# Soft-MoE routing behind beacon attention: logits in four column groups, dispatch turned on VectorE, combine rows replicated at the output

## Chip, cores and metric

The kernel runs on one core of a Trainium2 chip. The metric is the device time of one execution in microseconds; the number shown for a kernel is the median of its runs. A profile is of one execution, and its span runs from the first to the last instruction.

## The reference, cut to what matters

```python
# attention: B, H, S, Nb, D = 8, 8, 576, 16, 64
k_all = np.concatenate([beacon_k, k], axis=2)
v_all = np.concatenate([beacon_v, v], axis=2)
scores = 1/np.sqrt(D) * np.matmul(q, k_all.transpose(0, 1, 3, 2))
scores = np.where(causal, -1e9, scores)        # beacons are always seen
a = softmax(scores)                            # over the keys
x = np.matmul(a, v_all)                        # -> (B*S, H*D) = (4608, 512)
# soft MoE: 8 experts, 4 slots each (32 slots), F = 1024
logits = x @ phi                               # (4608, 32)
d = softmax(logits, over tokens)               # dispatch
slot_input = d.T @ x                           # (32, 512), 4 rows per expert
slot_out[e] = np.maximum(slot_input[e] @ w1[e], 0) @ w2[e]
c = softmax(logits, over slots)                # combine
return c @ slot_out                            # (4608, 512), fp32
```

The dispatch normalization needs the logits of all tokens of all batches, so the experts start only after the last attention output. The kernel takes the exponential of the logits once and without a maximum; dispatch and combine both use it, and divide by the sums over tokens (`dsum`, `rd`) and over slots (`csp`, `rc`).

## The kernel before

**Attention.** The 64 heads go in 32 pairs, `n` = 0 to 31; four pairs make a batch (`b, g = divmod(n, 4)`). A pair's tokens, 16 beacons ahead of 576, are five chunks of 128 (the last 80). Q and K are loaded by SP in fp32 into five rotating buffers of `arena`; `transp` turns them on PE (L265), and VectorE or ScalarE copies the result to `qT` and `kT` (L269, L271); GpSimd copies the beacons' K (L258). `score` has four stages `s0` to `s3`: matmuls into one of two double banks `scs` (L282), one exponential on ScalarE (L289), and the causal mask on GpSimd (L291). `attend_head` multiplies by V with a column of ones (L304) into `av`, and `normalize` (L314, L315) writes fp16 tokens-by-features `xb`. V is loaded by GpSimd and cast; VectorE turns it block by block (`turn_v`, L151, four calls per batch).

**Routing.** `xt_piece` turns `xb` on PE (L330) to features-by-tokens `xT` (L338). `logit_piece` multiplies by `phih`, which holds phi four times side by side, so that the 128 output partitions are the 32 slots four times (L344, 288 tokens at a time); ScalarE writes the exponential to `eLh` and the sum over tokens to `dsum9` (L348). `dt_piece` turns 32 rows of `eLh` on PE (L356), and VectorE copies them to tokens-by-slots `dT` (L361 to L363). `si_products` multiplies `dT` by `xb` in four column groups (L382), and `add_si` adds to `siacc` on VectorE (L388). `col_sums` sums over the slots with a column of ones (L416).

**Order.** The kernel is scheduled by hand: each engine runs its instructions in the order of the program text. Steps 0 to 5 are written out in `head(n)`; from step 6 on a step is the list of operations in L529, run by `step`. Logits of a batch are taken in steps 2 and 3 of the next, its dispatch in step 0 of the one after, its slot product in step 1; for the last two batches they are earlier. PSUM tiles of `ps_tr` (tag `tr`) rotate over two buffers. Expert weights are loaded by GpSimd, so many per step (`want`, L561).

**Tail.** After the last step the last pair is attended in `scs[0]` and normalized, its tokens are turned, the last logits are taken, and the dispatch and slot product of batch 7 follow (`si_half`, L370), added to the folded `siacc` (`fold_si`, L397) into `siz` (L616). `warm_tail` keeps PE busy between. Then come two layers of experts, two at a time (`first_layer` L642, `turn_hidden` L650, `second_layer` L656), and the scaled slot outputs `soh` (L675).

**Output.** For each group `cg` of 512 tokens four matmuls (L687) multiply columns of `eLh`, all 128 partitions, by `soh`, whose four partition groups hold partial sums of the slots; ScalarE (L689) and VectorE (L691) scale by `rc` in turn, and SP stores 1 MB (L695, L697).

Of the kernel before, what the change touches and what calls it, by code (L numbers as in the profile page):

```python
# [17 lines left out]
def kernel(  # L18
# [13 lines left out]
    P = 128  # L32
# [181 lines left out]
    nc.vector.memset(ones[:, :], 1.0)  # L214
# [8 lines left out]
    eLh = const.tile([P, Nb + N + P - UL], F16, name="eLh")  # L223
    nc.vector.memset(eLh[:, Nb + N:], 0.0)
    nc.vector.memset(eLh[:, 0:Nb], 0.0)
    dsum9 = const.tile([P, 2 * B - 1], FP, name="dsum9")
    siz = const.tile([P, E, NDC, NSL], F16, name="siz")
    fold = const.tile([P, NSL], FP, name="fold")
    siT = const.tile([P, NDC, NSL], FP, name="siT")
    phih = const.tile([P, NDC, 4, NSL], F16, name="phih")  # L230
# [89 lines left out]
    xT = {}  # L320
    dT = {}

    def xt_piece(n, act=False):
        b, g = divmod(n, H // 2)
        if g == 0:
            xT[b] = exq.tile([P, NDC, U], F16, name="xT", tag="xT", bufs=2)
        tp = ps_tr.tile([P, NCH, P], F16, name="tr", tag="tr")
        for i in range(NCH):
            m = P if i < 4 else UL
            nc.tensor.transpose(  # L330
                tp[:, i, 0:m],
                xb[b % 2][0:m, i, 2 * g:2 * g + 2, :].rearrange("p h d -> p (h d)"),
                idh[0:m, 0:m])
        src = tp[:, :, :].rearrange("p i u -> p (i u)")[:, 0:U]
        if act:
            nc.scalar.activation(xT[b][:, g, :], src, AF.Copy)
        else:
            nc.vector.tensor_copy(out=xT[b][:, g, :], in_=src)  # L338

    def logit_piece(b, hf):  # L340
        lp = ps_tr.tile([P, 512], FP, name="tr", tag="tr")
        w = S // 2
        for t in range(NDC):
            nc.tensor.matmul(lp[:, 0:w], phih[:, t, :, :].rearrange("p g s -> p (g s)"),  # L344
                             xT[b][:, t, Nb + hf * w:Nb + (hf + 1) * w],
                             start=(t == 0), stop=(t == NDC - 1))
        o = Nb + b * S + hf * w
        nc.scalar.activation(eLh[:, o:o + w], lp[:, 0:w], AF.Exp,  # L348
                             accum_out=dsum9[:, 2 * b + hf:2 * b + hf + 1])

    def dt_piece(b):
        dT[b] = sml.tile([P, NCH, NSL], F16, name="dT", tag="dT", bufs=2)
        tp = ps_tr.tile([P, NCH, NSL], F16, name="tr", tag="tr")
        for i in range(NCH):
            m = P if i < 4 or b == B - 1 else UL
            nc.tensor.transpose(tp[0:m, i, :], eLh[0:NSL, b * S + P * i:b * S + P * i + m],  # L356
                                idh[0:NSL, 0:NSL])
        if b == B - 1:
            nc.vector.tensor_copy(out=dT[b][:, :, :], in_=tp[:, :, :])
        else:  # L360
            nc.vector.tensor_copy(out=dT[b][:, 0:4, :], in_=tp[:, 0:4, :])  # L361
            nc.vector.tensor_copy(out=dT[b][0:UL, 4, :], in_=tp[0:UL, 4, :])
        nc.vector.memset(dT[b][0:Nb, 0, :], 0.0)  # L363
# [43 lines left out]
    csp = av[:, 0, 400:512]  # L407
    rc = const.tile([P, NG * G], FP, name="rc")

    def etok(cg, j):  # L410
        o = Nb + cg * P * G
        return eLh[:, o:o + P * G].rearrange("p (t j) -> p t j", j=G)[:, :, j]

    def col_sums(c0, c1):
        for i in range(c0 * G, c1 * G):
            nc.tensor.matmul(csp[:, i:i + 1], etok(i // G, i % G)[0:NSL], ones[0:NSL, :],  # L416
                             start=True, stop=True)

    def head(n):
# [5 lines left out]
        for x, y in {1: ((0, 0), (0, 1)), 3: ((1, 1),), 4: ((1, 0), (1, 2))}.get(n, ()):  # L425
            turn_v(x, y)
# [31 lines left out]
        if n >= 2:  # L458
# [4 lines left out]
            normalize(x)  # L463
        if n == 4:
# [10 lines left out]
    def step(op, n, b, g):  # L475
        m = n + 2
        last = b == B - 1
# [13 lines left out]
        elif op == "C" and g == 2 and b > 1:  # L491
            col_sums(b - 2, b - 1)
# [6 lines left out]
        elif op == "lg" and not last and g > 1:  # L499
            logit_piece(b - 1, g - 2)  # L500
        elif op == "lL" and last and 0 < g < 3:
            logit_piece(b - 1, g - 1)
        elif op == "dt":
            if g == 0 and b > 1:
                dt_piece(b - 2)
            if n == NP - 1:
                dt_piece(b - 1)
        elif op == "si":
            if g == 1 and b > 1:
                add_si(si_products(b - 2))  # L510
            if n == NP - 1:
                add_si(si_products(b - 1))
# [11 lines left out]
    for n in range(NP):  # L524
# [3 lines left out]
        else:  # L528
            for op in ("s0", "s1", "Tq", "Tk", "s2", "V", "C", "a0", "dt", "s3", "lg", "xt", "lL",  # L529
                       "si", "a1"):  # L530
                step(op, n, b, g)

        if n == 4:
            nc.gpsimd.tensor_copy(out=phih[:, :, :, :],
                                  in_=phif[:, :, :].unsqueeze(2).broadcast_to([P, NDC, 4, NSL]))
# [5 lines left out]
        if n == 16:  # L541
            nc.gpsimd.tensor_copy(out=fold[:, :], in_=idb[:, 0:NSL])
            for z in range(1, 4):
                nc.gpsimd.tensor_tensor(out=fold[:, :], in0=fold[:, :],
                                        in1=idb[:, NSL * z:NSL * z + NSL], op=AL.add)
            nc.gpsimd.tensor_scalar(out=fold[:, :], in0=fold[:, :], scalar1=2.0 ** -8,
# [22 lines left out]
    def col_sum_factors():  # L569
        nc.vector.tensor_scalar(out=rc[:, :], in0=csp[:, 0:NG * G], scalar1=2.0 ** 8,  # L570
                                scalar2=None, op0=AL.mult)
        nc.vector.reciprocal(out=rc[:, :], in_=rc[:, :])

# [3 lines left out]
    for rows in ((4,), (3, 2, 1), (0,)):  # L577
        for a in range(2):
# [3 lines left out]
    lps = [scs[1][:, hf, 0:S // 2] for hf in range(2)]  # L582

    def last_logits(ts):
        for hf in range(2):
            for t in ts:
                o = Nb + hf * (S // 2)
                nc.tensor.matmul(lps[hf], phih[:, t, :, :].rearrange("p g s -> p (g s)"),
                                 xT[L][:, t, o:o + S // 2],
                                 start=(t == 0), stop=(t == NDC - 1))  # L590

    last_logits([0, 1])
    fold_si(0)
    xt_piece(NP - 1)
    last_logits([2])
    fold_si(1)
    last_logits([3])
    for hf in range(2):
        o = Nb + L * S + hf * (S // 2)
        nc.scalar.activation(eLh[:, o:o + S // 2], lps[hf], AF.Exp)  # L600
    col_sums(6, 7)

    def warm_tail(k):
        for _ in range(k):
            nc.tensor.matmul(scs[0][:, 1, :], idh[:, :], xT[L][:, 0, 0:512],
                             start=True, stop=True)

    warm_tail(3)
    dt_piece(L)
    warm_tail(2)  # L610
    ds = siz[:, :, :, :]
    for hf in range(2):
        sp = si_half(L, hf)
        for r in range(2):
# [8 lines left out]
    dsum = const.tile([P, 1], FP, name="dsum")  # L623
    rd = const.tile([P, 1], FP, name="rd")
    nc.vector.reduce_sum(out=dsum9[:, 2 * L:2 * L + 1], in_=eLh[:, Nb + L * S:Nb + N],
                         axis=mybir.AxisListType.X)
    nc.vector.reduce_sum(out=dsum[:, :], in_=dsum9[:, :], axis=mybir.AxisListType.X)
    nc.vector.tensor_scalar(out=dsum[:, :], in0=dsum[:, :], scalar1=2.0 ** -16, scalar2=None,
                            op0=AL.mult)
    nc.vector.reciprocal(out=rd[:, :], in_=dsum[:, :])  # L630
# [31 lines left out]
    for p in range(EP + 2):  # L662
        if p < EP:
            first_layer(p)
        if p == 1:
            col_sums(7, NG)
            col_sum_factors()
# [12 lines left out]
    for cg in range(NG):  # L680
# [15 lines left out]
        if cg > 0:  # L696
            nc.sync.dma_start(out=dst, in_=osb[:, :, :])  # L697

# [29 lines left out]
```

## Time and profile before

| | us |
|---|---|
| median of 4 runs (194.45 to 196.72) | 195.99 |
| the profiled execution | 196.72 |
| its span | 194.7 |
| busy: PE / VectorE / ScalarE / GpSimd | 156.4 / 136.4 / 130.2 / 111.1 |
| start of score 0 of pair 31 | 146.58 |
| end of the loop's last `av` matmuls | 150.87 |
| first layer starts | 157.12 |
| `soh` starts | 166.39 |
| first output issued by SP | 168.26 |
| last VectorE copy of the output ends | 180.2 |

How to read it: PE is TensorE's matmul unit, PEld its weight load, DVE VectorE, ACT ScalarE, POOL GpSimd, SP the engine that issues loads and stores. A row of a group of instructions gives line, engine, operation, output and input with shapes, the count, busy time and mean ns of one. In the timeline a line gives start, duration, engine, line, operation and, in brackets, the idle time ahead of it and who ended it. An engine that is idle costs time only if the work that sets the end stands behind it.

### The profile page before, as it was taken

What the parts mean: (1) busy time and instruction counts of PE and PEld (TensorE: products, weight loads), DVE (VectorE), ACT (ScalarE), POOL (GpSimd) and SP (SyncE); (2) the same over time, 40 slices, a digit from 0 to 9 for tenths busy, and PEclk for the clock granted to TensorE, in tenths of its full rate; (3) what the DMA queues carried; (4) which work ended last, traced back from release to release, by engine and by line L of the source; (5) the groups of instructions that cost most, each with busy time, mean ns of one, the idle gap of its engine ahead of it and who ended that gap; (6) DMA issues with size and microseconds to landing.
All of it is one profiled execution on the core that took longest, in us unless ns stands there. A gap on an engine that the chain in (4) does not pass through costs nothing.

```text
span 194.7 us, 7205 instructions
## 1 busy us (share of the span) xinstructions
PE 156.4 (80%) x3061; PEld 107.5 (55%) x3061; DVE 136.4 (70%) x283; ACT 130.2 (67%) x190; POOL 111.1 (57%) x285
## 2 busy tenths in 40 slices
PE   6688958899899789997988899899988999787000
PEld 2345746667667557775766577577655754332000
DVE  5348378699978789997878779889845552799000
ACT  2679744689969678886878698698978222598000
POOL 8659847697887587769857766677646200000000
PEclk9955888999999999999999999999999999999655
DMA  5999999999999999999999999999999991199995
GB/s 192 247 225 333 291 242 318 259 268 266 289 262 265 263 295 274 271 255 315 258 259 264 284 290 268 274 205 169 215 214 214 214 211 32 56 404 416 417 426 226
DMA packets 20464, 50.84 MB, mean 261 GB/s; under 512 B 5456, under 2 KB 5456, under 8 KB 19408
## 3 DMA queue, kind: packets, MB, share of 16 engines
q0 software_dynamic: 8048, 21.74, 56.8%
q1 hardware_dynamic: 12240, 28.35, 40.1%
q8 instruction: 24, 0.39, 0.8%
q10 hardware_dynamic: 144, 0.29, 0.5%
q14 instruction: 8, 0.07, 0.1%
HBM read 62.65 MB, written 9.44 MB: 370 GB/s over the span
## 4 chain that ended last, share of the span: by engine, by line
PE 48%; DMA 18%; DVE 8%; ACT 8%; issue 5%; POOL 3%; SPq 1%; DVEq 0%; ACTq 0%
DMA arena<-in_k_dram 14%; PE av L304 14%; PE sc L282 12%; ACT ex L289 7%; PE tr L330 4%; PE tr L265 4%; DMA vbuf<-in_v_dram 4%; PE tr L344 3%; DVE arena L691 3%; PE av L656 2%; PE sc L642 2%; DVE xb L315 2%; PE tr L382 2%; POOL ex L291 1%; PE fp L687 1%
## 5 line engine op out<-in xcount | busy, mean ns | idle before, releaser
L289 ACT ACTIVATE ex<-sc 128x736 f16<-128x736 f32 (+1 forms) x124 | 101.9, 870 | 30.2 <-PE sc L282 26.2
L291 POOL TENSOR_SCALAR_AFFINE_SELECT ex<-ex 128x256 f16<-128x256 f16 (+1 forms) x155 | 57.9, 400 | 34.9 <-ACT ex L289 34.4
L282 PE MATMUL sc<-qT,kT 64*128 64x336 bf16 (+5 forms) x384 | 43.4, 296 | 9.7 <-ACT ex L289 4.1
L304 PEld LDWEIGHTS <-ex 128*128 128x128 f16 (+1 forms) x930 | 36.0, 107 | 12.3 <-issue 11.6
L304 PE MATMUL av<-vh,ex 128*128 128x65 f16 x840 | 38.3, 198 | 3.6 <-DVE xb L315 1.8
L265 PE MATMUL tr<-idb,arena 64*64 64x64 bf16 x1152 | 28.3, 200 | 5.3 <-DMA arena<-in_k_dram 2.7
L265 PEld LDWEIGHTS <-arena 64*64 64x64 bf16 x1152 | 23.4, 113 | 13.5 <-issue 9.0
L271 DVE COPY qT<-tr 128x576 bf16<-128x576 bf16 x32 | 24.0, 749 | 5.9 <-PE tr L265 5.8
L315 DVE TENSOR_TENSOR xb<-av,r 128x640 f16<-128x640 f32 x31 | 25.6, 824 | 1.1
L282 PEld LDWEIGHTS <-kT 64*128 64x128 bf16 (+1 forms) x384 | 16.5, 101 | 16.8 <-issue 6.5
L338 DVE COPY xT<-tr 128x592 f16<-128x592 f16 x31 | 14.1, 460 | 13.0 <-PE tr L330 12.8
L151 DVE STREAM_TRANSPOSE vh<-vbuf 128x256 f32<-128x256 f32 x32 | 20.4, 659 | 3.2 <-DMA vbuf<-in_v_dram 3.1
L271 DVE COPY kT<-tr 128x576 bf16<-128x576 bf16 x27 | 20.2, 750 | 3.3 <-PE tr L265 3.3
L183 POOL DMA_DIRECT2D arena<-in_moe_w_dram x32 | 17.9, 560 | 0.2
L127 POOL DMA_DIRECT2D vbuf<-in_v_dram x27 | 15.1, 571 | 0.2
L689 ACT ACTIVATE arena<-fp,rc 128x512 f32<-128x512 f32 (+1 forms) x18 | 11.4, 676 | 4.7 <-PE fp L687 4.0
L330 PE MATMUL tr<-idh,xb 128*128 128x128 f16 (+1 forms) x160 | 13.9, 222 | 0.2 <-DVE xb L315 0.2
L691 DVE TENSOR_SCALAR arena<-fp,rc 128x512 f32<-128x512 f32 (+1 forms) x19 | 12.5, 731 | 0.4 <-PE fp L687 0.4
L330 PEld LDWEIGHTS <-xb 128*128 128x128 f16 (+1 forms) x160 | 10.5, 101 | 4.1 <-issue 3.2
L687 PE MATMUL fp<-soh,eLh 128*128 128x512 f16 (+1 forms) x37 | 10.8, 371 | 2.2 <-ACT arena L689 1.5
L344 PE MATMUL tr<-xT,phih 128*128 128x288 f16 x56 | 9.4, 288 | 0.2 <-DVE xT L338 0.2
L314 DVE RECIPROCAL r<-av 128x10 f32<-128x10 f32 x31 | 6.8, 220 | 3.3 <-PE av L304 2.5
(99 smaller groups left out, 134.7 us busy)
## 6 DMA issues: line engine op xcount, KB each, us to landing
arena<-in_moe_w_dram POOLq DMA_DIRECT2D x32, 512.0 KB, 9.7
arena<-in_q_dram SPq DMA_DIRECT2D x32, 288.0 KB, 14.2
arena<-in_k_dram SPq DMA_DIRECT2D x31, 288.0 KB, 14.9
out_dram<-arena SPq DMA_DIRECT2D x8, 1024.0 KB, 9.7
vbuf<-in_v_dram POOLq DMA_DIRECT2D x30, 128.0 KB, 7.8
arena<-in_v_dram POOLq DMA_DIRECT2D x4, 128.0 KB, 7.4
out_dram<-arena SPq DMA_DIRECT2D x2, 256.0 KB, 3.1
out_dram<-arena SPq DMA_DIRECT2D x1, 512.0 KB, 3.1
```

Of the source, the lines that this page charges most:

```text
L151: nc.vector.transpose(out=dst[:, e], in_=src.bitcast(FP).rearrange("p (j e) -> p e j", j=TK)[:, e])
L183: nc.gpsimd.dma_start(out=arena[:, wloc[m]:wloc[m] + WP], in_=src)
L265: nc.tensor.transpose(tp[po:po + 64, j, :], hi, idb[po:po + 64, po:po + 64])
L271: nc.vector.tensor_copy(out=dst, in_=src)
L282: nc.tensor.matmul(sc[0:kn, a, col:col + un], kT[n % 3][64 * a:64 * a + 64, P * c:P * c + kn], qT[n % 3][64 * a:64 * a + 64, u0:u0 + un], ...
L289: nc.scalar.activation(e, sc[:, :, 0:w], AF.Exp, scale=scale)
L291: nc.gpsimd.affine_select(out=e[0:m, :, o:o + m], in_=e[0:m, :, o:o + m], compare_op=AL.is_ge, fill=0.0, base=0, pattern=[[0, 2], [1, m]], ...
L304: nc.tensor.matmul(dst[0:m, i * DD:(i + 1) * DD], ex[n][0:kn, o + a * w:o + a * w + m], vchunk(b, 2 * g + a, c, kn), start=(c == 0), stop= ...
L315: nc.vector.tensor_tensor(out=xb[b % 2][:, :, 2 * g:2 * g + 2, :].rearrange("p i a d -> p a i d"), in0=avv[:, :, :, 0:D], in1=r5[:, :, :]. ...
L330: nc.tensor.transpose(tp[:, i, 0:m], xb[b % 2][0:m, i, 2 * g:2 * g + 2, :].rearrange("p h d -> p (h d)"), idh[0:m, 0:m])
L344: nc.tensor.matmul(lp[:, 0:w], phih[:, t, :, :].rearrange("p g s -> p (g s)"), xT[b][:, t, Nb + hf * w:Nb + (hf + 1) * w], start=(t == 0), ...
L691: nc.vector.tensor_scalar(out=osb[:, j, c], in0=fp_[:, c], scalar1=rc[:, i:i + 1], scalar2=None, op0=AL.mult)
```

## The change

- The logits of a batch are one tile of 128 x 160: phi is the 32-column weight, and four column groups `z` of PE take runs of 32 tokens each. Partition 32z + s holds slot s; column 32i + q is token 128i + 32z + q. `xT` becomes two fixed tiles with a zeroed tail, since the runs of the last chunk go past token 592.
- One exponential writes it to `eLz`, a region at the end of `eLh`; the sums over tokens are no longer taken there, but in one VectorE sum over all of `eLz` at the end (`dsz`), and a matmul with a replicated `fold` adds the four groups (`slot_factors`).
- `dT` comes from one VectorE transpose in blocks of 32 x 32.
- `eLh` as the output needs it, slots four times in order of tokens, is made later: `spread_rows` (chunks 0 to 3) and `spread_ends` (the last 80 tokens) multiply `eLz` by `rept` on PE and copy from PSUM. Batches 0 and 1 and the ends of 0 to 3 are made in the tail, the others between the groups of the output; `col_sums` and the reciprocal go there too, group by group.
- The order of a step becomes `s0 s1 Tq Tk s2 V a0 lg s3 dt xt si a1`; logits and dispatch of the batch before are in step 2, its slot product in step 3. In the tail both folds come ahead of the last `xt_piece`, `warm_tail` is gone, and three GpSimd memsets clear the unused columns of `eLz`.
- `turn_v(1, 1)` goes from the middle of step 3 to its end.

```diff
-    eLh = const.tile([P, Nb + N + P - UL], F16, name="eLh")
+    ZW = NCH * 32
+    zo = N + 64 - B * ZW
+    eLh = const.tile([P, N + 64], F16, name="eLh")
+    eLz = eLh[:, zo:zo + B * ZW].rearrange("p (b i q) -> p b i q", b=B, q=32)
+    xTs = [const.tile([P, NDC * U + 48], F16, name=f"xT{i}") for i in range(2)]
-    phih = const.tile([P, NDC, 4, NSL], F16, name="phih")
+    phih = const.tile([P, NDC, NSL], F16, name="phih")
-    def logit_piece(b, hf):
...
+    def logits(b, lp, ts):
+        x = xTs[b % 2][:, :]
+        for t in ts:
+            for z in range(4):
+                nc.tensor.matmul(
+                    lp[32 * z:32 * z + NSL, :], phih[:, t, :],
+                    bass.AP(tensor=x.tensor, offset=x.offset + t * U + 32 * z,
+                            ap=[x.ap[0], [P, NCH], [1, 32]]),
+                    start=(t == 0), stop=(t == NDC - 1), tile_position=(0, 32 * z))
+    def logit_exp(b, lp):
+        nc.scalar.activation(eLz[:, b].rearrange("p i q -> p (i q)"), lp, AF.Exp)
     def dt_piece(b):
...
+        nc.vector.transpose(out=dT[b][:, :, :].rearrange("p i s -> p (i s)"),
+                            in_=eLz[:, b].rearrange("p i q -> p (i q)"))
+        nc.vector.memset(dT[b][0:Nb, 0, :], 0.0)
+    def spread_rows(b, eng):
+        sp = ps_tr.tile([P, 4, 4, 32], FP, name="tr", tag="tr")
+        for z in range(4):
+            spread(sp[:, :, z, :], z, eLz[:, b, 0:4, :])
+        evac(eng, eLh[:, b * S:b * S + 4 * P - Nb],
+             sp[:, :, :, :].rearrange("p i z q -> p (i z q)")[:, Nb:])
+    def spread_ends(b0, b1, eng, sp=None):
...
+        for z in range(3):
+            w = min(32, UL - 32 * z)
+            spread(spv[:, :, 32 * z:32 * z + w], z, eLz[:, b0:b1, 4, 0:w])
+        evac(eng, eLh[:, b0 * S:b1 * S].rearrange("p (b s) -> p b s", s=S)[:, :, S - UL:], spv)
     def col_sums(c0, c1):
...
+        nc.vector.reciprocal(out=rc[:, c], in_=csp[:, c])
-            for op in ("s0", "s1", "Tq", "Tk", "s2", "V", "C", "a0", "dt", "s3", "lg", "xt", "lL",
-                       "si", "a1"):
+            for op in ("s0", "s1", "Tq", "Tk", "s2", "V", "a0", "lg", "s3", "dt", "xt", "si", "a1"):
+            for z in range(4):
+                nc.gpsimd.tensor_copy(
+                    out=rept[:, z, :, :],
+                    in_=idb[:, NSL * z:NSL * z + NSL].unsqueeze(1).broadcast_to([P, 4, NSL]))
     for rows in ((4,), (3, 2, 1), (0,)):
+        if rows == (0,):
+            spread_rows(0, nc.vector)
...
-    last_logits([0, 1])
+    lp = scs[1][:, 0, 0:ZW]
+    logits(L, lp, [0, 1, 2])
     fold_si(0)
+    fold_si(1)
     xt_piece(NP - 1)
-    last_logits([2])
-    fold_si(1)
-    last_logits([3])
...
-    col_sums(6, 7)
-    warm_tail(3)
+    logits(L, lp, [3])
+    logit_exp(L, lp)
+    spread_rows(1, nc.scalar)
     dt_piece(L)
-    warm_tail(2)
+    nc.gpsimd.memset(eLz[64:96, :, 4, UL - 64:32], 0.0)
+    nc.gpsimd.memset(eLz[96:P, :, 4, :], 0.0)
+    nc.gpsimd.memset(eLz[0:32, :, 0, 0:Nb], 0.0)
...
+    spread_ends(0, 4, nc.scalar, av[:, 1, 128:128 + 4 * UL])
+    nc.vector.reduce_sum(out=dsz[:, :], in_=eLz.rearrange("p b i q -> p (b i q)"),
+                         axis=mybir.AxisListType.X)
         if p == 1:
-            col_sums(7, NG)
-            col_sum_factors()
+            col_sums(0, 1)
+            slot_factors()
         if cg > 0:
             nc.sync.dma_start(out=dst, in_=osb[:, :, :])
+        if cg + 2 < B:
+            spread_rows(cg + 2, (nc.scalar, nc.vector)[cg % 2])
+        if cg == 1:
+            spread_ends(4, B - 1, nc.scalar)
+        if cg == 5:
+            spread_ends(B - 1, B, nc.scalar)
+        if cg + 1 < NG:
+            col_sums(cg + 1, cg + 2)
```

## Prediction

> **What bounds the kernel now.** I read the page first, then the waits, then the timeline by steps. From the page:
>
> ```profile
> span 194.7 us, 7205 instructions
> PE 156.4 (80%) x3061; PEld 107.5 (55%) x3061; DVE 136.4 (70%) x283; ACT 130.2 (67%) x190; POOL 111.1 (57%) x285
> DMA  5999999999999999999999999999999991199995
> HBM read 62.65 MB, written 9.44 MB: 370 GB/s over the span
> ```
>
> Read the DMA row first: full from the second slice to 160 us, two slices nearly empty, full again to the end. The inputs keep the DMA busy to about 160 us; the output (9.44 MB at 419 GB/s in the window 172 to 180) takes the last 22.5 us. Between them stands the tail of compute. So the end is set by when the first output leaves, and time is gained only if the slot outputs `soh` are ready earlier.
>
> The waits of PE on loads, from the timeline of PE:
>
> ```profile
> 64.91 0.47 PE L265 MATMUL tr<-idb,arena 64*64 64x64 bf16 x18 [0.23 <-DMA arena<-in_k_dram]
> 70.66 0.47 PE L265 MATMUL tr<-idb,arena 64*64 64x64 bf16 x18 [0.94 <-DMA arena<-in_k_dram]
> ```
>
> After the start these are the only waits of PE on K loads. SP's K loads were issued at 51.07 and 55.77 for pairs 15 and 16, and pair 15 landed at 70.66: there the compute has caught up with the loads. A gain made before 70 us is lost here. Afterwards nothing waits for K (Q once, 0.2 us).
>
> At the start VectorE stands before a turn of V of batch 1, and PE's next scores behind it:
>
> ```profile
> 25.47 0.66 DVE L151 STREAM_TRANSPOSE vh<-vbuf 128x256 f32<-128x256 f32 x1 [3.07 <-DMA vbuf<-in_v_dram]
> 27.08 0.35 PE L282 MATMUL sc<-qT,kT 64*128 64x80 bf16 x4 [2.29 <-POOL kT L258]
> ```
>
> From 75 us the steps (one pair of heads) are bound by PE, VectorE and ScalarE in turn. By the starts of score 0 a batch of four takes 17.24 us (pairs 20 to 23, 99.60 to 116.84) and 16.77 us (24 to 27). Step 29, with a logit piece and the slot product in one, is long (137.67 to 142.51, 4.84 us), and shows why:
>
> ```profile
> 141.37 0.61 PE L382 MATMUL tr<-xb,dT 128*32 128x512 f16 x5
> 141.48 0.41 ACT L348 ACTIVATE eLh<-tr 128x288 f16<-128x288 f32 x1 [0.18 <-PE tr L344]
> 141.78 0.20 ACT L348 ACTIVATION_READ_ACCUMULATOR eLh<-tr 128x1 f32 x1
> 142.02 0.69 DVE L388 TENSOR_TENSOR siacc<-siacc,tr 128x512 f32<-128x512 f32 x1 [0.91 <-PE tr L382]
> ```
>
> The tail, where each line waits for the one before (the timeline):
>
> ```profile
> 152.24 0.82 DVE L315 TENSOR_TENSOR xb<-sc,r 128x640 f16<-128x640 f32 x1
> 153.20 0.42 PE L330 MATMUL tr<-idh,xb 128*128 128x128 f16 x5
> 153.67 0.47 DVE L338 COPY xT<-tr 128x592 f16<-128x592 f16 x1 [0.61 <-PE tr L330]
> 154.63 0.71 ACT L600 ACTIVATE eLh<-sc 128x288 f16<-128x288 f32 x2 [1.44 <-PE sc L588]
> 156.34 0.67 PE L370 MATMUL tr<-dT,xb 128*128 128x32 f16 x20
> 157.12 1.91 PE L642 MATMUL sc<-arena,siz 128*32 128x512 f16 x32
> ```
>
> From the end of the loop's last `av` matmuls (150.87) to the first layer are 6.25 us, and 9.3 us more to `soh` (166.39).
>
> [...] the 20 slot matmuls of 32 columns (L370) take 0.67 us, 33 ns each with the last one's latency. [...] The tail's new pauses are about 1 us each, so I charge nothing for the removed warming matmuls.
>
> **The change, part by part.**
>
> *Logits.* Removed per batch: two pieces of four matmuls of 128x288, 0.49 us of the chain each, and on ScalarE two exponentials of 0.40 us with a 0.20 us read of the sum. Added: 16 matmuls of 160 columns in four column groups. The first layer does the same with 512 columns: 64 in 4.0 us, 61 ns each, so the groups overlap; at 160 columns the spacing rules, which in L656's weight loads is 34 ns (16 in 0.55 us). So 0.55 us, and one exponential of 128x160, some 0.30 us by size. [...] I take 0.55.
>
> *Dispatch.* Removed: five transposes on PE (0.23 us of the chain) and two copies on VectorE (0.19 + 0.16). Added: one VectorE transpose of 128x160, [...] bounds 0.24 (the copy of as many elements, L359) and 0.45 (the rate of the 32-bit turn). VectorE neither wins nor loses. But it waits for the exponential, and behind it stand xT's copy, `r` and `xb`.
>
> *Column sums.* Four matmuls per batch (0.21 us of the chain) leave the loop.
>
> PE saves 0.49 x 2 + 0.23 + 0.21 - 0.55 = 0.87 us per batch. VectorE does not: per step qT 0.75, kT 0.75, turn 0.66, xT 0.47, r 0.22, xb 0.82 = 3.67 us, so 4 x 3.67 + 0.42 + 0.69 = 15.8 us per batch, against 16.8 to 17.2 measured. PE also loses about 1 us pauses named "issue" (0.61 at 104.04, 0.79 at 110.07) that stay. In step 2 of a batch the logits now go ahead of score 3, so its exponential is 0.5 us later, and the next score 1, in the same bank, waits about 0.1 us. I take 0.6 us saved per batch for the two and a half batches from pair 18 to 27: 1.5 us. Pairs 13 to 17 carry the tail turns (VectorE 9.81 us busy of 80 to 90): nothing saved.
>
> *Pairs 28 to 31.* Step 29 loses the logit piece, the slot product (0.54 us) and its addition (0.69): 4.84 becomes 3.6. Step 28 loses 0.23 of dispatch, step 31 the same; step 30 is held by ScalarE's four exponentials (3.41 us) and stays. 1.24 + 0.23 + 0.23 = 1.7 us.
>
> *V of batch 1.* VectorE's 3.07 us go, and PE's 2.29; what is late next is pair 15's K at 70.66. Kept: 0 (bounds 0 and 2.0).
>
> *`rept` on GpSimd*, four copies of 128x128, 0.3 us each (the 128x512 cast took 0.61): GpSimd already holds PE for 0.2 us there (`fold`), its masks and DMA issues queue behind. I charge 0.3 (0 to 1.0).
>
> Loop: 1.5 + 1.7 - 0.3 = 2.9 us earlier.
>
> *The tail to the first layer.* VectorE gets a copy of `spread_rows(0)` ahead of the last pair's normalize: 496 elements from PSUM, 0.63 us (the 128x512 eviction of L691 took 0.73 with its scale), and it waits for PE, so `xb` is 0.8 late. Then PE does both folds (0.8 us) ahead of the last transposes instead of one, and VectorE `siT` (0.29) ahead of xT's copy: another 0.3. Then gains: the last logits 0.25 instead of 0.41, the exponential 0.30 instead of 0.71; and PE's five transposes, the copy from PSUM and the warming matmuls give way to VectorE's 0.35. Then a new wait: `spread_ends(0, 4)` stands on PE ahead of the slot product and reads what two GpSimd memsets write, which follow VectorE's transpose: 0.4 us plus 0.25 for its matmuls. From xT's copy: matmuls 0.05 + 0.23, exponential 0.03 + 0.30, transpose and memset 0.05 + 0.42, GpSimd 0.40, spread 0.30, so 1.75 us to the slot product, against 2.2 (154.14 to 156.34). Sum 0.8 + 0.3 - 0.45 = 0.65 us later.
>
> *The experts.* VectorE's sum over 1280 elements is 1.65 us (576 took 0.74), done as the first two first layers end (1.91); hidden. The fp32 factor matmul (0.4) takes the place of four column sums (0.2): 0.2 us later.
>
> *The output.* Copies of 0.6 us for six batches, three each on ScalarE and VectorE, two for the ends, a reciprocal per group. VectorE's group takes 1.37 us now, 2.2 with them, and the DMA 2.5 us per MB: hidden, but for the first groups, where a reciprocal delays the second MB: 0.2 us.
>
> Sum: -2.9 + 0.65 + 0.2 + 0.2 = -1.85, rounded to -2.0 for step 13's lost addition: the profiled execution (196.72, span 194.7 and 2.0 around it) would be 194.7. The median of the runs, 195.99, is 0.73 below it: 194.0.
>
> **Does a weight become the bound?** The DMA's share is 0.76 in 159 to 162 and 0.05 after, so the last weights land at about 161; the last expert's matmuls start at 165.9. A tail up to 4.5 us earlier still finds them loaded.
>
> **Rivals.** (a) The start's gain is kept: pair 15's K, issued earlier, lands earlier too, at the cost of weights. For it: weights have slack. Against: the DMA was full throughout. 2 us more: 192.0. (b) The loop stays with VectorE at its sum, and only the last four pairs gain: 194.0 + 1.5 = 195.5. For it: 9.81 us of 10 at 80 to 90. Against: 7.10 at 90 to 100. (c) The other side: VectorE stands before dT's transpose, since ScalarE takes the logit exponential only after exponential 2; xT, `r` and `xb` queue behind, and PE's next `av` waits for `xb`. Up to 0.8 us in each of the five batches past pair 13: 4.0 us, so 198.0. It decides from 0.4 us per batch. Against: exponential 2 ends 2.9 us into a step, VectorE's turn at 3.25.
>
> **How the numbers follow.** A measurement of this kernel tells about 1% from no change (1.96 us). The forecast has 0.44, own range 192.8 to 195.4: 0.24 faster, 0.18 within, 0.02 slower. (a) 0.18, all faster. (b) 0.16: 0.04 faster, 0.12 within. (c) 0.22: 0.06 within, 0.16 slower. Faster 0.46, same 0.36, slower 0.18. The range 191.6 to 197.6 takes in most of (a) and the lower half of (c).
>
> **What would show it.** Right: PE waits for K near 65 to 71 us by more than 1.2 us, score 0 of pair 31 starts near 143.9 instead of 146.58, the first layer near 154.9, the first output near 166.1 instead of 168.26. Wrong: VectorE idle before dT's transpose by over 0.4 us a batch; score 0 of pair 31 later than 145.5; logits over 1 us; a halved clock in the tail; DMA gaps in the output.

## The result and the profile after

The changed kernel has a median of 198.35 us in 36 runs (195.25 to 206.63); the kernel before had 195.70 in 57 runs on the same chip (193.33 to 200.16). The ratio is 1.0084, 95% interval 1.0061 to 1.0107, which is 1.65 us slower; the two medians lie 2.65 us apart. Medians here are of all runs; ratios leave out the runs of either kernel that lie more than 1.5% above its fastest, so where times spread widely the two can disagree. The profiled execution took 199.69 us, with a span of 197.9; that is 1.3 us above the median, but e3 and e4, whose tails have the same code, show the same fall of the clock there (3.61 us for the first layer in both) in executions near their medians (198.06 and 199.25).

The page of the changed kernel; the row PEclk is TensorE's granted clock in tenths of full speed, for 40 slices of 4.95 us:

```profile
span 197.9 us, 7324 instructions
PE 159.9 (81%) x3123; PEld 108.8 (55%) x3123; DVE 140.0 (71%) x286; ACT 128.2 (65%) x175; POOL 112.3 (57%) x293
PEclk9955999759999996999999999799999559999955
DMA  5999999999999999999999999999999940289995
HBM read 62.65 MB, written 9.44 MB: 364 GB/s over the span
```

The same row of the kernel before, which the prediction did not show:

```profile
PEclk9955888999999999999999999999999999999655
```

Busy times say little: PE 3.5 us more, VectorE 3.6 more. The clock row says where to look. In the kernel before, the clock is at full from 31.0 to 181.2 us, that is until PE's work is done. In the changed kernel there are dips, and the widest (the fives in slices 32 and 33) lies over the tail and the experts. The half clock lasts from 153.6 to 163.9, 10.2 us; the three shorter ones take 37.6 to 44.4 (6.8 us), 75.1 to 78.6 (3.4) and 122.9 to 126.3 (3.4).

The way to the end, step by step, in the two profiled executions:

| | before | after | difference | forecast |
|---|---|---|---|---|
| score 0 of pair 31 starts | 146.58 | 144.50 | -2.08 | -2.7 |
| loop's last `av` matmuls end | 150.87 | 148.58 | -2.29 | -2.9 |
| from there to the first layer | 6.25 | 7.30 | +1.05 | +0.65 |
| first layer to first output matmuls | 9.81 | 13.74 | **+3.93** | +0.2 |
| from there to the end of the span | 27.77 | 28.28 | +0.51 | +0.2 |
| span | 194.7 | 197.9 | +3.2 | -1.85 |

One row carries the result. The timeline of PE in the changed kernel's tail (L346 logits, L367 spreads, L651 first layer, L635 factor matmul in fp32):

```profile
153.13 0.25 PE L346 MATMUL sc<-xT,phih 128*32 128x160 f16 x4 [0.56 <-DVE xT L340]
153.31 0.40 PE L367 MATMUL tr<-eLh,rept 128*128 128x128 f16 x4
154.83 0.43 PE L367 MATMUL av<-eLh,rept 128*128 128x128 f16 x3 [1.11 <-POOL eLh L612]
155.88 3.60 PE L651 MATMUL sc<-arena,siz 128*32 128x512 f16 x32
160.14 0.56 PE L635 MATMUL av<-dsz,qT 128*128 128x1 f32 x2 [0.44 <-DVE rc L447]
```

The 32 matmuls of the first layer take 3.60 us; the kernel before needed 1.91. No PE pause in this tail is longer than 1.11 us, and the clock has already fallen when that pause begins. The busy time by stretches of 3.4 us, as long as the shortest of these dips, counted backwards and forwards from the fall, shows what differs. Columns: PE, PEld, DVE, ACT and POOL busy with instruction counts, then granted clock, DMA share, GB/s. First the changed kernel; then the kernel before, at the same time and 2.29 us later, which is the same stage, since its loop ended by so much later:

```profile
150.20:153.60 3.40, 2.34 (x33) 1.85 (x34) 1.92 (x5) 0.83 (x2) 0.00 (x0) 1.00 1.07 216
153.60:157.00 3.40, 2.19 (x37) 1.38 (x38) 1.78 (x7) 1.16 (x3) 0.94 (x4) 0.51 1.06 213
157.00:160.40 3.40, 2.96 (x30) 1.13 (x23) 0.69 (x2) 1.19 (x2) 0.00 (x0) 0.50 0.96 193
160.40:163.80 3.40, 3.40 (x30) 1.41 (x33) 1.00 (x4) 0.60 (x1) 0.00 (x0) 0.50 0.17 34
```

```profile
150.20:153.60 3.40, 3.21 (x66) 2.98 (x66) 2.72 (x6) 0.91 (x2) 1.49 (x3) 1.00 1.07 216
152.49:155.89 3.40, 3.35 (x35) 2.46 (x33) 1.33 (x3) 1.38 (x3) 0.00 (x0) 1.00 1.05 212
```

Behind a stretch in which PE was busy 2.34 of 3.40 us the clock was halved; it came back behind one busy 3.40 of 3.40. The kernel before has 3.21 and 3.35 us busy. `warm_tail` has no part in the first figure and about 0.9 us in the second: its five matmuls stand at 154.84 to 156.41, behind the last logits. In the changed kernel that place comes only at the end of the stretch ahead of the fall, since its last `xT` is later. So two causes stand side by side here, the missing fill and the new tail; e2 and e11 below part them.

### The profile page after: what moved, and what is told of

It is laid out like the page before. It is cut to its first block, busy times and chain, and to the rows that moved or that the text cites. A ratio compares the mean times of both kernels' runs of the same rounds, so it can differ in the third digit from the quotient of the medians.

```text
span 197.9 us, 7324 instructions
## 1 busy us (share of the span) xinstructions
PE 159.9 (81%) x3123; PEld 108.8 (55%) x3123; DVE 140.0 (71%) x286; ACT 128.2 (65%) x175; POOL 112.3 (57%) x293
## 5 line engine op out<-in xcount | busy, mean ns | idle before, releaser
L287 PE MATMUL sc<-qT,kT 64*128 64x336 bf16 (+5 forms) x384 | 45.7, 303 | 6.8 <-ACT ex L294 3.0
L309 PEld LDWEIGHTS <-ex 128*128 128x128 f16 (+1 forms) x930 | 38.2, 110 | 16.0 <-issue 14.0
L309 PE MATMUL av<-vh,ex 128*128 128x65 f16 x840 | 40.6, 202 | 5.8 <-issue 3.2
L270 PE MATMUL tr<-idb,arena 64*64 64x64 bf16 x1152 | 29.0, 201 | 6.0 <-DMA arena<-in_k_dram 2.3
L270 PEld LDWEIGHTS <-arena 64*64 64x64 bf16 x1152 | 24.0, 115 | 14.5 <-issue 8.6
L332 PE MATMUL tr<-idh,xb 128*128 128x128 f16 (+1 forms) x160 | 14.4, 225 | 0.0
L700 DVE TENSOR_SCALAR arena<-fp,rc 128x512 f32<-128x512 f32 (+1 forms) x19 | 13.1, 732 | 1.2 <-PE fp L696 0.4
L332 PEld LDWEIGHTS <-xb 128*128 128x128 f16 (+1 forms) x160 | 9.7, 102 | 6.7 <-issue 6.5
L654 ACT ACTIVATE hbuf<-sc 128x512 f16<-128x512 f32 x4 | 2.4, 597 | 8.1 <-PE sc L651 8.1
```

Of the source, the lines that this page charges most:

```text
L270: nc.tensor.transpose(tp[po:po + 64, j, :], hi, idb[po:po + 64, po:po + 64])
L287: nc.tensor.matmul(sc[0:kn, a, col:col + un], kT[n % 3][64 * a:64 * a + 64, P * c:P * c + kn], qT[n % 3][64 * a:64 * a + 64, u0:u0 + un], ...
L309: nc.tensor.matmul(dst[0:m, i * DD:(i + 1) * DD], ex[n][0:kn, o + a * w:o + a * w + m], vchunk(b, 2 * g + a, c, kn), start=(c == 0), stop= ...
L332: nc.tensor.transpose(tp[:, i, 0:m], xb[b % 2][0:m, i, 2 * g:2 * g + 2, :].rearrange("p h d -> p (h d)"), idh[0:m, 0:m])
```

## The experiments

The theories: (1) the loop and the tail went about as forecast, and the fall of the clock in the tail, where `warm_tail` is gone, turned a gain into a loss; (2) the start lost time, since GpSimd stood before phi's load; (3) the turn of V that was moved later gains at the start what is lost again by 70 us, or does harm; (4) the order of the tail costs the time, whatever the clock.

**e1: the fill put back.** The changed kernel with eight filling matmuls of 512 columns where PE pauses.

```diff
-    logits(L, lp, [0, 1, 2])
...
+    logits(L, lp, [0, 1])
+    warm_tail(2)
+    logits(L, lp, [2])
     fold_si(0)
     fold_si(1)
     xt_piece(NP - 1)
+    warm_tail(2)
     logits(L, lp, [3])
     logit_exp(L, lp)
     spread_rows(1, nc.scalar)
+    warm_tail(4)
```

> The changed kernel with eight warming matmuls put back in the tail: two between the last logits' pieces, two ahead of the last piece, four behind spread_rows(1). Theory 1 (the tail's clock): in the changed kernel PE's granted clock falls to 0.5 at 153.6 us and stays there for 10 us, so that the first layer takes 3.60 us for 32 matmuls instead of 1.91; with PE kept busy the clock stays at 1.0 from 150 to 165, the first layer to soh takes 9.3 us again instead of 13.2, and the kernel gains 3 to 4 us on the changed one: 194.5 to 195.5 by the median. Rival (the pauses are the same with or without the fill, the clock falls by load elsewhere): the clock still halves and the gain is under 1 us.

Measured: median 196.22, where the kernel before had 196.54, ratio 0.9999 (0.9966 to 1.0031). In the profiled execution (203.21 us, at half clock from 141.1 to 151.3, ahead of the tail: 14 `av` matmuls take 1.00 us there and 0.63 after) the clock in the tail stays at full, the first layer takes 1.91 us, and from it to the first output matmuls 10.38 us instead of 13.74. The loss is gone, by 0.85% of ratio or some 1.7 us on the changed kernel instead of the 3 to 4 expected; a gain on the kernel before does not appear. The fill's own tile cost time: its first pair waited 0.30 us for the normalize that reads the same bank, so the first layer came 8.15 us after the loop.

**e5: the same fill into a bank that nobody reads** (`scs[1]` instead of `scs[0]`).

> The changed kernel with the eight warming matmuls of e1, but written to the second bank of scs[1], which nothing reads then, instead of scs[0], which the last pair's normalize reads: in e1 the first two waited for normalize, and the first layer came 8.15 us after the loop's last av matmuls instead of 7.30. Theory 1 (clock): granted clock 1.0 from 150 to 165, 7.3 us from the last av matmuls to the first layer, 10.4 us from there to the first output matmul (changed kernel 13.7): 3.4 us better than the changed kernel in the tail, about 194.0 by the median, 0.6 to 1.0 us better than e1. Rival (the fill costs as much as it saves): no better than e1, 195.5 to 196.

Measured: median 195.41, where the kernel before had 195.86, ratio 1.0000 (0.9967 to 1.0034), so no better than e1 beyond the intervals, with a span of 191.9 in the profile. PE in its tail:

```profile
151.99 1.02 PE L606 MATMUL sc<-xT,idh 128*128 128x512 f16 x4
153.94 1.91 PE L661 MATMUL sc<-arena,siz 128*32 128x512 f16 x32
156.50 0.35 PE L645 MATMUL av<-dsz,qT 128*128 128x1 f32 x2 [0.44 <-DVE rc L447]
```

L661 is the first layer at full clock. It starts 7.81 us after the loop, so the fill costs some 0.5 us of its own against 7.30, and the way on is again 10.38: 0.57 more than before, at the same clock.

**e2: the kernel before, without its fill.** The two calls of `warm_tail` are deleted, and nothing else.

> The kernel before with its two groups of warming matmuls (3 and 2) removed and nothing else. Theory 1: they alone hold the clock in the tail; without them it halves somewhere between 154 and 165 and the kernel is 2 to 4 us slower than before (198 to 200). Rival (it is the new tail with its column groups, fp32 folds in a row and the wait for GpSimd that lets the clock fall): the kernel before keeps its clock, and the time stays within 0.5 us, 195.3 to 196.3.

Measured: median 196.78, where the kernel before had 196.54, ratio 1.0040 (1.0008 to 1.0071): slower, but by some 0.8 us and not by 2 to 4. The profile shows the same mechanism in the old code:

```profile
155.57 0.71 PE L370 MATMUL tr<-dT,xb 128*128 128x32 f16 x20 [0.47 <-DVE dT L363]
156.37 3.11 PE L640 MATMUL sc<-arena,siz 128*32 128x512 f16 x32
```

The first layer comes 6.02 us after the loop, 0.23 us earlier than with fill, then takes 3.11 instead of 1.91, with the clock at half from 155.4 to 158.8. That is 3.4 us, where the changed kernel has 10.2; PE was busy 2.67 of the 3.40 us ahead of the fall (2.34 there) and 3.24 of the next 3.40 (2.19 there). So the same deletion costs 0.4% there.

**e11: fill at the longest pause only.** Four matmuls after `spread_rows(1)`, where PE waits 1.11 us for GpSimd.

> The changed kernel with four filling matmuls at one place alone, after the spread of batch 1's reciprocals, where PE pauses 1.11 us for GpSimd. It tells which pause costs the clock. Theory A (the density of PE's work ahead of that pause decides, since in the changed kernel the clock fell at 153.7, ahead of it): the clock still falls near the last transposes[...], the first layer takes more than 2.5 us, ratio 1.003 to 1.008. Theory B (the 1.11 us pause decides): clock at full through the tail, first layer 1.9 us, ratio 0.998 to 1.001 as with the whole fill.

Measured: median 196.81, where the kernel before had 195.66, ratio 0.9958 (0.9916 to 1.0). The profile bears out theory A on the clock; the stretch ahead of the fall, and the fill behind it:

```profile
149.60:153.00 3.40, 2.33 (x35) 1.77 (x33) 2.15 (x5) 0.66 (x1) 0.00 (x0) 1.00 1.06 213
```

```profile
153.42 1.87 PE L606 MATMUL sc<-xT,idh 128*128 128x512 f16 x4
```

PE was busy 2.33 of the 3.40 us before, the clock fell at 153.0, and the four filling matmuls then ran at half speed: 1.87 us against 1.02 in e5. With them PE was busy 3.31 of the next 3.40 us (2.19 in the changed kernel), and the clock came back at 156.4, so the first layer was hurt only in its first tenths (2.02 us). The time does not decide: the ratio lies below the range of both theories, while the median is 0.6% above that of the kernel before.

**e3: phi's cast one step later.** In the changed kernel GpSimd stood 5.13 us before phi's load, since compute had got ahead of it; the masks, the beacon copies and the DMA issues stood behind. The timeline of the changed kernel:

```profile
34.69 0.29 POOL L554 CAST phih<-phif 128x128 f16<-128x128 f32 x1 [5.13 <-DMA phif<-in_moe_phi_dram]
...
38.47 0.53 PE L287 MATMUL sc<-qT,kT 64*128 64x80 bf16 x4 [1.80 <-POOL kT L263]
...
74.57 0.47 PE L270 MATMUL tr<-idb,arena 64*64 64x64 bf16 x18 [1.72 <-DMA arena<-in_k_dram]
```

```diff
-        if n == 4:
+        if n == 5:
             nc.gpsimd.tensor_copy(out=phih[:, :, :], in_=phif[:, :, :])
```

> The changed kernel with the cast of phi on GpSimd one step later (after step 5 instead of 4). Theory 2 (the start's gain is lost at phi): in the changed kernel GpSimd stands 5.13 us before phi's load, and the beacons' copies and masks behind it hold PE for 1.8 us at 38.47; with the cast later that wait goes, score 0 of step 6 starts at about 36.4 instead of 38.5, the clock does not fall at 38 us, and what is kept at the end is 0 to 2 us. Rival (K of pair 15 bounds at 70 us whatever comes before, as forecast): step 6 starts 2 us earlier, but PE waits for K by as much more near 65 to 75, and the time stays within 0.7 us of the changed kernel's.

Measured: median 197.77, ratio 1.0032 (0.9997 to 1.0067). The wait for GpSimd is gone: score 0 of step 6 starts at 36.34, as in the changed kernel (36.37), but its second half no longer stands until 38.47. K takes part of that back:

```profile
52.46 0.47 PE L270 MATMUL tr<-idb,arena 64*64 64x64 bf16 x18 [2.42 <-DMA arena<-in_k_dram]
```

The half clock in the tail is there again, from 152.4 to 162.6, with 13.80 us from the first layer to the output matmuls. The median is 0.6 us below the changed kernel's, within the 0.7 that the rival allows; the loop of the profile ends 1.42 us earlier (147.16), so a part of the wait may be kept.

**e6: e5 with phi's cast one step later.**

> e5 with the cast of phi one step later (as e3). Theory 2 (GpSimd's wait for phi costs the loop something that K's loads do not take back): the loop ends 0.5 to 1.4 us earlier than in e5 (e3 ended it at 147.16, the changed kernel at 148.58), so 193 to 193.5. Rival (K's loads near 50 to 75 us take it back): within 0.4 us of e5.

Measured: median 196.42, where the kernel before had 195.86, ratio 1.0034 (1.0005 to 1.0063), so no better than e5; the median is 1.0 us above e5's. PE waits for K 1.43 us at 38.40, 1.85 at 69.36 and 1.35 at 74.43. Theory 2 names a real wait, but one that another takes over.

**e4: the turn of V put back into the middle of step 3**, in the changed kernel.

```diff
-        for x, y in {1: ((0, 0), (0, 1)), 4: ((1, 0), (1, 2))}.get(n, ()):
+        for x, y in {1: ((0, 0), (0, 1)), 3: ((1, 1),), 4: ((1, 0), (1, 2))}.get(n, ()):
...
-        if n == 3:
-            turn_v(1, 1)
```

> The changed kernel with turn_v(1, 1) back in the middle of step 3. Theory 3 (the later turn is lost again by 70 us): VectorE's 3 us wait is back at 22 to 25 us, GpSimd no longer stands before phi, and the time is within 0.7 us of the changed kernel's. Rival (the later turn does harm: getting ahead of phi and of K's loads makes PE pause by 1.8 us and lets its clock fall to 0.5 from 37 to 45 us): without it the clock dip at 37 to 45 us is gone and the kernel is 1 to 2 us faster than the changed one.

Measured: median 198.99 in 6 runs, ratio 1.0101 (1.0036 to 1.0166), within 0.7 us of the changed kernel as theory 3 has it. The half clock at 37 to 45 us is gone, but another lies at 27.0 to 30.4 (ten transposes take 1.07 us at 26.90, 0.69 at 34.67), and the rival's 1 to 2 us do not appear. PE waits 2.00 us at 25.56 again, and K costs 0.42 us instead of 1.72: the last `av` of the loop end at 148.26, against 148.58 with the turn moved.

**e8: the converse, the kernel before with the turn moved late.**

> The kernel before with turn_v(1, 1) moved to the end of step 3 and nothing else. Forecast's theory (K of pair 15 takes it back): VectorE's 3 us wait at 22 to 25 us is gone, step 5 starts 2 to 3.4 us earlier than 34.25, GpSimd stands before phi at about 30 to 34 us and gives it back by step 6, and the time is within 0.4 us of before. Rival (part of it is kept): 0.5 to 2 us faster than before. Third (PE's pause behind phi lets its clock fall): up to 1 us slower.

Measured: median 196.06, where the kernel before had 195.86, ratio 1.0029 (0.9997 to 1.0062). The start is 4 us ahead (step 5 at 30.21, where the other order had 34.25), and K takes it:

```profile
51.35 0.47 PE L265 MATMUL tr<-idb,arena 64*64 64x64 bf16 x18 [1.96 <-DMA arena<-in_k_dram]
70.25 0.47 PE L265 MATMUL tr<-idb,arena 64*64 64x64 bf16 x18 [1.67 <-DMA arena<-in_k_dram]
```

Together with a wait of 1.02 us for Q at 35.34 nearly all is gone: the loop ends at 150.83, against 150.87. Moving the turn alone is worth nothing.

**e7: e6 with the tail straightened in three places.** The spread of batch 0 is copied by ScalarE, the second fold comes after the last transposes, and the spread of the ends after the slot product.

```diff
-            spread_rows(0, nc.vector)
+            spread_rows(0, nc.scalar)
...
     fold_si(0)
-    fold_si(1)
     xt_piece(NP - 1)
+    fold_si(1)
...
```

> e6 with three changes of order in the tail: the first spread_rows evicted by ScalarE instead of VectorE, the last pair's transposes between the two folds as before, and spread_ends(0, 4) behind the slot product instead of ahead of it, so that the slot product does not stand behind GpSimd's memsets. Theory 4 (the tail's added microsecond is these three): from the last av matmuls to the first layer 5.3 to 5.8 us instead of 7.3 (before: 6.25), so 1.5 to 2 us better than e6: 191.5 to 192. Rival (another wait takes their place, the exponential or the weights' landing at 161): less than 0.7 us better than e6.

Measured: median 195.17 in 14 runs, where the kernel before had 195.86, ratio 0.9998 (0.9963 to 1.0033). The first layer came 7.03 us after the loop, not within the range expected: filling matmuls and the logits that wait for `xT` stand in PE's order ahead of the last transposes. As a gain it is inconclusive.

**e9: the tail reordered, no fill.**

```diff
...
-    logits(L, lp, [0, 1, 2])
-    fold_si(0)
-    fold_si(1)
+    logits(L, lp, [0, 1])
+    spread_rows(0, nc.scalar,
+                scs[1][:, 1, :].rearrange("p (i z q) -> p i z q", i=4, z=4))
     xt_piece(NP - 1)
+    logits(L, lp, [2])
+    fold_si(0)
     logits(L, lp, [3])
     logit_exp(L, lp)
+    fold_si(1)
     spread_rows(1, nc.scalar)
     dt_piece(L)
...
-    spread_ends(0, 4, nc.scalar, av[:, 1, 128:128 + 4 * UL])
...
+    spread_ends(0, 4, nc.scalar, av[:, 1, 128:128 + 4 * UL])
     nc.vector.reduce_sum(out=dsz[:, :], in_=eLz.rearrange("p b i q -> p (b i q)"),
...
```

> The changed kernel with its tail in another order and no filling matmuls: the spread of batch 0's reciprocals is copied by ScalarE, not by VectorE ahead of the last normalize; both folds of the slot accumulators come after the last transposes and the first logits; the spread of the ends after the slot product; each expert's factor matmul ahead of its first column sums. Theory (order costs the tail its time, and the clock is a second, separate cost): from the end of the last av matmuls to the first layer 5.2 to 5.6 us instead of 7.30; if the granted clock holds at full in the tail, the first layer takes 1.9 us and the way from it to the first expert's second-layer matmuls 9.9 us, so 192.5 to 193.5 us and a ratio to the kernel before of 0.983 to 0.989; if the clock falls as in the changed kernel, the way is 13.3 us, 196 to 197 us, ratio about 1.001. Rival (the order is hidden by ScalarE and by the DMA of the weights): the first layer starts as in the changed kernel, 7.0 us or more after the last av, and the ratio is that of the changed kernel, 1.008.

Measured: median 197.40 in 14 runs, where the kernel before had 195.66, ratio 0.9997 (0.9931 to 1.0063): 0.9% slower by the medians and equal by the ratio, so the time does not decide. The first layer starts 6.74 us after the loop: 0.56 better than 7.30, but outside the theory's 5.2 to 5.6, since PE still waits 0.51 us for `xT` and 0.41 for ScalarE's copy. Order alone does not hold the clock, which fell at 157.0, so that the first layer took 3.53 us:

```profile
153.60:157.00 3.40, 2.99 (x47) 2.41 (x50) 1.31 (x8) 1.00 (x4) 0.93 (x4) 1.00 1.06 212
```

```profile
156.88 3.53 PE L652 MATMUL sc<-arena,siz 128*32 128x512 f16 x32
```

Here PE counts as busy 2.99 of 3.40 us, a share of 0.88, mostly in matmuls of 32 and 160 columns and in fp32, and the clock fell all the same. So the share of busy time in the profile does not tell by itself when the clock falls; the stretches of other runs stand below, under "What stood ahead of the falls".

**e10 and e12: the reordered tail with two filling matmuls, and with five.** In e10 they stand after `spread_rows(1)`; e12 has three there and two after the last transposes. (The 5.75 us in e12's expectation is counted from the end of the last pair's own matmuls; in the count used elsewhere it is 6.74.)

> The same reordered tail, with two filling matmuls of 512 columns into an idle bank of PSUM while PE waits for the transpose of dT. Theory: the fill stands beside a wait, so it costs at most 0.3 us; first layer 5.3 to 5.9 us after the last av matmuls; with the clock held, 1.9 us for the first layer, 192.5 to 194 us, ratio 0.983 to 0.991. Rival (two matmuls of 0.22 us are too little to keep the clock): [...] the first layer 3 us or more, ratio 1.00 to 1.01.

> The reordered tail with five filling matmuls of 512 columns instead of two: two after the last transposes, where PE waits 0.41 us for ScalarE's copy, and three while PE waits for the transpose of dT. In the profile of the kernel with two, the first layer came 5.75 us after the last av matmuls, and the first expert's second-layer matmuls 10.28 us after that. Theory (the median is held up by executions in which the clock still falls in the tail, and more fill makes those fewer): mean granted clock of the runs 0.933 to 0.94 instead of 0.928, first layer 5.7 to 6.1 us after the last av matmuls, median 194.5 to 195.5 us, ratio to the kernel before 0.990 to 0.996. Rival (the spread of the runs comes from the loop's own half-clock stretches and K loads, not from the tail): mean clock 0.925 to 0.931, median 195.5 to 196.5 us, ratio 0.994 to 1.001.

Measured: e10 has median 196.12 where the kernel before had 195.66, ratio 0.9936 (0.9898 to 0.9974); e12 has median 195.33 where the kernel before had 196.49, ratio 1.0006 (0.9971 to 1.0041). Both profiles keep the clock in the tail, with 1.91 us for the first layer, which starts 6.74 and 6.83 us after the loop and 10.28 us on to the output. In e10 the way to the first layer and the ratio came out worse than the theory had them, the ratio better than the rival's. In e12 the first layer and the median lay in the theory's range, the ratio and the mean clock of the runs, 0.930, in the rival's. The interval of e10 is below 1, though its median is above that of the kernel before, and the interval of e12 holds 1, with more fill and otherwise nearly the same code; so the two together do not show a version that beats the kernel before.

**The clock of all runs.** Each run gives its mean granted clock:

| no fill in the tail | clock | with fill | clock |
|---|---|---|---|
| changed kernel | 0.913 | e5 / e1 | 0.935 / 0.924 |
| e3 | 0.915 | e6 / e7 | 0.929 / 0.929 |
| e4 | 0.907 | e10 / e12 / e11 | 0.928 / 0.930 / 0.925 |
| e9 | 0.911 | kernel before (four sets) / e8 | 0.925 to 0.929 / 0.929 |
| e2 (old tail) | 0.923 | | |

The four changed kernels without fill lie lowest, apart from all the others. Within a kernel, a run with 0.01 less clock takes 1.09 us more (269 runs of the twelve experiments and the changed kernel, 95% interval 0.95 to 1.22). The changed kernel has 0.0147 less than the mean of the four sets of before, 0.9273: by that slope 1.6 us, about the whole of the 1.65 measured by the ratio. A correlation is not a cause by itself; e1 and e5, which changed only the fill, are the test.

## Why the prediction was wrong

It said 194.0 us; the sign was wrong. A halved clock in the tail stood among its signs of being wrong, but without a price. Rival (c)'s 198.0 came near the measured 198.35 by luck, since its mechanism held nobody up. Point by point:

- **The step that failed** is "The tail's new pauses are about 1 us each, so I charge nothing for the removed warming matmuls." The pauses were indeed 0.51, 0.56 and 1.11 us. But the clock fell ahead of the third, at 153.6, behind a stretch busy 2.34 of 3.40 us that holds the first two; and the removed matmuls were work at that stage, 0.90 us of the 3.35 in the kernel before. The fall cost 3.36 us in the profiled execution (13.74 against 10.38 in e5) and about 1.6 us over the runs. The step looked at the length of each pause alone. That pauses of about 1 us leave the clock at full was the author's assumption, which no run had shown: half clock came behind a stretch busy 2.34 of 3.40 us, with no pause over 0.56 in it.
- **The loop's sum** was near right, by parts that were not. In the eight changed profiles in which no half clock fell into the last steps (all but e1, e7 and e9), score 0 of pair 31 starts at 143.46 on average, in the three of the old loop (before, e2, e8) at 146.39: 2.9 earlier, forecast 2.7 at that point. But the pairs 28 to 31 gained 1.40 us (12.98 to 11.58), not 1.7; the pairs 18 to 27 gained 0.53 (44.04 to 43.51), not 1.5; and 0.98 came from ahead of pair 18, where the step had a loss of 0.3. In the pairs 18 to 27 rival (b) was largely right: most of PE's saved time did not shorten the batch. Half clock in these pairs takes a part: in the profiles without any there, two of the old loop and four of the new, the gain is 0.76 (43.86 to 43.10).
- **The costs of the new operations** came out. The timeline of the changed kernel in a step with logits:

```profile
109.89 0.46 PE L346 MATMUL tr<-xT,phih 128*32 128x160 f16 x16
...
110.40 0.30 ACT L353 ACTIVATE eLh<-tr 128x160 f16<-128x160 f32 x1 [1.31 <-PE tr L346]
...
110.74 0.35 DVE L362 STREAM_TRANSPOSE dT<-eLh 128x160 f16<-128x160 f16 x1 [1.24 <-ACT eLh L353]
```

  The logits took 0.46 us (0.55 was taken), the exponential 0.30 (0.30), the transpose 0.35 (0.35, the author's estimate, which no run had shown).
- **Rival (c)** falls, though its mark came: VectorE stands 1.24 us here before the transpose, 5.5 us in six steps over the whole span. Between 89 and 148 us no wait of PE is put down to VectorE in the changed kernel, so nobody stood behind it.
- **The start's gain** was rightly counted as lost in the profiled execution: score 0 of pair 20 starts at 99.67, against 99.60. K was the cause at 74.57 (1.72 us), as forecast with a different place, 65 to 71. But GpSimd's 5.13 us before phi and PE's 1.80 behind it were not foreseen. Averaged over the profiles some of the gain stays, so rival (a) was partly right.
- **The tail** was charged 0.65 and cost 1.05. The last normalize's `xb` came 0.65 later after the loop (2.02 us instead of 1.37; 0.8 was charged). The folds and `siT` ahead of the last `xT` copy added another 0.58 (0.3 was charged). From that copy to the slot product 2.45 us instead of 2.67, a gain of 0.22 where 0.45 was counted.
- **The experts** were charged 0.2 and cost 0.57 at full clock. The factor matmul waits 0.44 us for the first reciprocal of `rc`, which stands ahead of it.
- **The output** was charged 0.2. From first output matmuls to the end the old output takes 27.77, 28.12 (e2) and 27.62 (e8), the new 28.28, 27.58 (e5), 28.20 (e10) and 27.72 (e12): no difference beyond the spread.

With measured sizes the sum without the clock is -2.9 + 1.05 + 0.57 = -1.3 us, within 1% of the kernel before; e5, whose fill costs 0.5 of that, should have gained 0.8, and had equal time to within 0.65: some of the sum does not show in the runs, and which part stays open. With the clock it is about +0.3 by the runs' slope (1.6), and +2.1 by the profiled tail (3.36); the measured 1.65 lies between them. The likeliest outcome was then "within 1%", and the clock decided the sign.

**What stood ahead of the falls.** PE's busy time in stretches of 3.40 us that end at a fall, and in stretches of the tail at full clock:

| run | stretch | PE busy, us | clock after it |
|---|---|---|---|
| changed kernel | 34.2 to 37.6 | 1.95 | half |
| changed kernel | 71.8 to 75.2 | 1.68 | half |
| changed kernel | 119.6 to 123.0 | 2.06 | half |
| changed kernel | 150.2 to 153.6 | 2.34 | half |
| e3 | 149.0 to 152.4 | 2.23 | half |
| e11 | 149.6 to 153.0 | 2.33 | half |
| e2 | 152.1 to 155.5 | 2.67 | half |
| e9 | 153.6 to 157.0 | 2.99 | half |
| e10 | 147.0 to 150.4 | 2.30 | full |
| e12 | 148.0 to 151.4 | 2.71 | full |
| e5 | 147.8 to 151.2 | 2.89 | full |
| kernel before | 151.9 to 155.3 | 3.19 | full |

Seven of the eight falls came behind 1.68 to 2.67 us, but busy time does not part the two groups: e9 lost the clock behind 2.99 us and e10 kept it behind 2.30. In e9's stretch stand 8 logit matmuls of 160 columns, 8 fp32 matmuls of 32, 20 slot matmuls of 32, 7 spreads of 128 and 4 matmuls of the first layer. What decides a fall was not shown; that the filling matmuls hold the clock in this tail was, by the profiles of e1, e5, e10 and e12. It was not tried to make the loop's own pauses shorter, in which the changed kernel's clock fell at 122.9.

## What to carry to other kernels

A filler that does nothing can be worth its time: deleting it alone made the first layer of the kernel before take 3.11 us instead of 1.91 (e2). Before deleting one, add up PE's busy time around it, short pauses together, and do not look at the longest pause alone: the clock fell behind a stretch busy 2.34 of 3.40 us whose longest pause was 0.56. The busy time is a hint and no proof (2.99 lost the clock in e9, 2.30 kept it in e10), so measure the kernel without the filler. Read the clock row of the page before any busy time: the first layer's matmuls, with the same count, took 1.9 times as long (3.60 us against 1.91) by the clock and not by a wait. And where a stage is fed by loads that just keep pace, an earlier start is given back, wholly or in part, at a later load; e3 (2.42 us for K at 52.46), e6 (1.85 at 69.36) and e8 (1.96 at 51.35) each showed it at another place.

## What the runs showed of the hardware that was not expected

- The half clock lasted 3.4, 6.8 and 10.2 us in the changed kernel, 3.4 in the tails of e2 (155.4 to 158.8) and e11 (153.0 to 156.4), and 10.2 in that of e3 (152.4 to 162.6).
- PE that was busy at half clock did not get it back at once: in the changed kernel the stretch from 157.0, busy 2.96 of 3.40 us, was followed by another at half clock, and full clock came behind the one from 160.4, busy 3.40; in e3 likewise behind 2.96 and 3.40. In e2 and e11 full clock came behind 3.24 and 3.31.
- The clock fell behind a stretch busy 2.99 of 3.40 us (e9) and stayed behind one busy 2.30 (e10).
- Four matmuls of 512 columns take 1.02 us at full clock (e5) and 1.87 at half (e11), and the 32 of the first layer 1.91 and 3.60, 1.83 and 1.88 times as long, so most of a factor of two arrives in the time of these matmuls.
